# Three of the last stores of a scan-and-adapters kernel, each made by a transfer of 120 and one of 8 partitions

## The chip, the cores and the metric

The kernel runs on one core of one Trainium2 chip. The metric is the time of one execution on the device in microseconds (us); lower is better. The median of three runs of the kernel before is 204.93 us (204.83 to 204.99). Profiles show one execution each.

## The reference

Two steps follow each other. The first is a linear recurrence over time, `h = a*h + b`, for 8 sequences of 6400 steps with 128 channels. Its result, taken as 51200 rows of 128, goes through a mixture of 8 adapters of rank 16, of which each row uses its two best.

```python
def _attn_ref(a, b):                    # a, b: 8 x 6400 x 128
    h = zeros((B, D))
    for t in range(S):
        h = a[:, t] * h + b[:, t]
        out[:, t] = h

def _moe_ref(x, w_gate, A, B):          # x: 51200 x 128, A: 8 x 128 x 16, B: 8 x 16 x 128
    logits = x @ w_gate
    topk = the two largest of the 8 logits;  w = softmax over these two
    delta = sum over the two experts e of  w_e * ((x @ A[e]) @ B[e])
    return x + delta
```

The inputs `a` and `b` are 26.2 MB each and the output is 26.2 MB, so 78.6 MB have to cross between the off-chip and the on-chip memory.

## The kernel before, in words

The 51200 rows are cut into 100 units of 512 rows (`NU = 100`, `UT = 512`). For each unit the `a` and `b` rows are loaded, turned by TensorE so that the channels lie on the 128 partitions (line 81), `a` is copied to the on-chip memory by ScalarE (line 474), and VectorE runs the scan along the free axis (line 493). TensorE then makes the logits and the products with all 8 `A` (line 77), the gates are worked out in groups of units by VectorE and GpSimd, the weighted products are turned and multiplied by `B`, and the sum with `x` in the accumulator `pO` is evicted to the tile `outt` (line 789), by ScalarE alone or, in the last ten units, by ScalarE and VectorE in turn.

`outt` has `NOUT = 24` slots of one unit. A store takes two neighbouring slots, 128 partitions x 2 x 2 KB = 512 KB, to the output; units 98 and 99 have a store of 256 KB each. In the output a unit's 512 rows lie as 128 partitions of 4 rows. There are 51 stores, numbered by the first unit `u0` = 0, 2, ..., 96, 98, 99. The store of `u0` waits for the evictions of its units and, as long as `u0 + HOLD` (20 units later) is under `FREE = 96`, for the scan of that later unit. So the stores run well behind the arithmetic, and at the end some of them are left over.

All loads and stores are issued on SyncE's queue (SP) in an order that a planner (`_Plan.schedule`) makes ahead of time from costs, keys and due times; a step that issues transfers is planned at 450 ns of SP for each transfer that it starts. `add_dma` registers such a step. Its inner `emit` starts the transfers at line 306, and each adds 16 to the semaphore of its slot when it has landed; the slot's semaphore value that users wait for is raised by 16 for each transfer. `_Plan.run` puts a wait at line 193 ahead of each step that needs one. The last instruction of SP, `end`, waits for the last 24 stores.

The line at which a store is described, before the change, is

```python
            rows = out[u0 * UT : (u0 + n) * UT, :].rearrange("(n p i) d -> p n (i d)", p=128, i=Q)
            ...
                [(rows, outt[:, s0 : s0 + n, :])],
```

Of the kernel before, what the change touches and what calls it, by code (L numbers as in the profile page):

```python
# [20 lines left out]
POOL_MULS = (0, 20, 4, 2)  # L21
HOLD = 20
FREE = 96
RING = 8
XR = 16
NOUT = 24
# [173 lines left out]
def bass_associative_scan_2x2__then__mixture_of_adapters_kernel(  # L200
# [20 lines left out]
    lo, hi, every, at = POOL_MULS  # L221
# [23 lines left out]
    with ExitStack() as stack:  # L245
# [11 lines left out]

        a_in = sb(nc.sbuf_tensor("a_in", [128, RING, QI * D], F32))
        b_in = sb(nc.sbuf_tensor("b_in", [128, RING, QI * D], F32))
        a_st = [sb(nc.sbuf_tensor(f"a_st{i}", [128, UT], F32)) for i in range(2)]  # L260
# [5 lines left out]
        outt = sb(nc.sbuf_tensor("outt", [128, NOUT, UT], F32))  # L266
# [30 lines left out]
        def add_dma(name, eng, unit, starts, slot, time, deps=()):  # L297

            if slot not in dma_sem:
                dma_sem[slot] = [sb(nc.semaphore("q_" + "_".join(map(str, slot)))), 0]  # L300
            dma_sem[slot][1] += 16 * len(starts)
            sem, value = dma_sem[slot]

            def emit(h):
                for dst, src in starts:
                    last = h.dma_start(dst, src).then_inc(sem, 16)
                return last

            add(name, eng, "dma", unit, (450.0 * len(starts), 0.0), emit, deps, (sem, value, time))
# [107 lines left out]
        def load(t, w):  # L417

            n = place(t, w)[0]
            many = 1 if (t, w) in alone else 2  # L420
            dst, i = rings[t][:, n % RING, :], QI
            if many == 1:
                dst, i = dst[:, column(t, w) : column(t, w) + UT], Q
            src = rows_of[t][w * UT : (w + many) * UT, :].rearrange("(p i) d -> p (i d)", i=i)
            for k in range(many):
# [3 lines left out]
                "sp",  # L429
                w - 2 * RING + (0 if w > 3 else -200),  # L430
                [(dst, src)],
                (t, n % RING, many, w if many == 1 else 0),
                650.0 if many == 1 else 1265.0,
                users.get((t, n - RING), []),
            )
# [369 lines left out]
        def store(j):  # L805
            u0, n = stores[j]
            s0 = u0 % NOUT
            rows = out[u0 * UT : (u0 + n) * UT, :].rearrange("(n p i) d -> p n (i d)", p=128, i=Q)
            add_dma(
                f"st{j}",  # L810
                "sp",
                u0 + HOLD,
                [(rows, outt[:, s0 : s0 + n, :])],
                ("o", s0, n),
                632.0 * n,
                [f"oev{v}" for v in range(u0, u0 + n)] + [f"scan{u0 + HOLD}"] * (u0 + HOLD < FREE),
            )
# [19 lines left out]
        for j in range(len(stores)):  # L837
            store(j)
# [53 lines left out]
```

## Time and profile before

| what | value |
|---|---|
| median of three runs | 204.93 us (204.83 to 204.99) |
| the profiled execution's own time | 204.77 us |
| its span, first to last instruction | 203.0 us |
| TensorE, VectorE, ScalarE, GpSimd busy | 93%, 91%, 85%, 57% of the span |
| moved by the transfer queues | 79.35 MB, mean 391 GB/s |
| stores | 49 of 512 KB, median 13.2 us from issue to landing; 2 of 256 KB, 4.6 us |
| mean granted TensorE clock | 0.982 |

The span is what the views show; the profiled execution's own time holds 1.8 us more around it. A transfer runs on up to 16 transfer engines side by side, and the DMA share is the mean over all 16, so one engine working alone shows as 0.06. A share can come out slightly over 1, since packets on an engine overlap by a few ns. "From issue to landing" ends with the last of a transfer's 16 landings. L306 and L193 are lines of helpers, so a store is best found by its place in time on SP.

### The profile page before, as it was taken

The numbers are of one execution on the slowest core, as the hardware profiler recorded it, in microseconds if no ns is written. First come the engines' busy times: TensorE is split into PE (matmuls) and PEld (weight loads), VectorE is DVE, ScalarE is ACT, GpSimd is POOL, SyncE is SP. The second block draws the span as 40 slices with busy tenths as digits, with TensorE's granted clock in tenths as the row PEclk, the third lists the DMA queues.
The fourth block names the chain that finished last, engine by engine and source line by source line (L and its number), as shares of the span: only waits on it lengthen the run. The fifth ranks groups of instructions, "written<-read, shape, count | busy, mean of one in ns | idle before, by whom it ended". The sixth has DMA issues, their size and how long they took to land.

```text
span 203.0 us, 8739 instructions
## 1 busy us (share of the span) xinstructions
PE 189.5 (93%) x3594; PEld 167.2 (82%) x3594; DVE 183.8 (91%) x260; ACT 172.8 (85%) x379; POOL 115.4 (57%) x240
## 2 busy tenths in 40 slices
PE   7788899998999999999999999999999999999970
PEld 2567788887889989988899889999998999889960
DVE  1599988999999999999999999999999999999960
ACT  2357498896979999999999999999999999898870
POOL 1326767655758565646656665575775654555610
PEclk9999699999999999999999999999999999999996
DMA  7999999999999999999999999999999999999884
GB/s 184 403 408 407 406 409 402 405 407 408 407 410 413 408 413 416 404 411 408 412 408 415 408 410 409 408 413 411 410 410 411 408 414 409 400 403 358 319 318 151
DMA packets 29671, 79.35 MB, mean 391 GB/s; under 512 B 3648, under 2 KB 3776, under 8 KB 29632
## 3 DMA queue, kind: packets, MB, share of 16 engines
q1 hardware_dynamic: 28304, 78.65, 98.3%
q8 instruction: 29, 0.48, 0.9%
q10 hardware_dynamic: 1328, 0.14, 0.5%
q14 instruction: 10, 0.08, 0.1%
HBM read 52.56 MB, written 26.21 MB: 388 GB/s over the span
## 4 chain that ended last, share of the span: by engine, by line
PE 85%; ACT 7%; DVE 2%; issue 2%
PE pA L81 28%; PE pO L77 22%; PE pTL L81 14%; PE pZ L77 11%; PE pTL L77 5%; PE pB L81 4%; ACT a_st L474 3%; PE pB L77 2%; DVE xT L493 2%; ACT zwT L750 2%; ACT outt L789 2%; ACT z_sb L698 1%; DVE outt L789 0%; ACT g L667 0%; DVE warm_t L355 0%
## 5 line engine op out<-in xcount | busy, mean ns | idle before, releaser
L493 DVE TENSOR_TENSOR_SCAN xT<-a_st,xT,pB 128x512 f16<-128x512 f32 x96 | 120.2, 1252 | 4.5 <-PE pTL L77 1.0
L474 ACT COPY a_st<-pA 128x512 f32<-128x512 f32 x100 | 60.9, 609 | 19.0 <-PE pB L81 15.3
L81 PE MATMUL pA<-ident_f,a_in 64*128 64x64 f32 (+1 forms) x792 | 72.1, 231 | 2.8 <-ACT a_st L474 1.2
L81 PE MATMUL pB<-ident_f,b_in 64*128 64x64 f32 (+1 forms) x792 | 72.6, 231 | 0.2
L81 PEld LDWEIGHTS pA<-ident_f,a_in 64*128 64x128 f32 (+1 forms) x792 | 58.0, 140 | 12.6 <-ACT a_st L474 2.9
L789 ACT COPY outt<-pO 128x512 f32<-128x512 f32 x95 | 59.6, 628 | 1.6 <-PE pO L77 1.4
L81 PEld LDWEIGHTS pB<-ident_f,b_in 64*128 64x128 f32 (+1 forms) x792 | 58.1, 140 | 0.7 <-issue 0.5
L750 ACT COPY zwT<-pTL 128x512 f16<-128x512 f16 x95 | 58.0, 611 | 0.2
L712 DVE TENSOR_TENSOR zw<-pZ,g 128x512 f16<-128x512 f32 x80 | 53.5, 672 | 0.8 <-PE pTL L81 0.2
L77 PE MATMUL pO<-ident_h,xT 128*128 128x128 f16 x400 | 38.6, 220 | 0.7 <-issue 0.3
L77 PE MATMUL pZ<-cst_h,xT 128*128 128x128 f16 x400 | 38.8, 221 | 0.1
L81 PE MATMUL pTL<-ident_h,zw 128*128 128x128 f16 x380 | 38.0, 223 | 0.5 <-issue 0.3
L77 PE MATMUL pO<-cst_h,zwT 128*128 128x128 f16 x400 | 38.1, 217 | 0.3 <-ACT zwT L750 0.3
L712 POOL TENSOR_TENSOR zw<-z_sb,g 128x512 f16<-128x512 f32 x20 | 21.3, 1063 | 17.2 <-PE pTL L77 15.0
L77 PEld LDWEIGHTS pO<-ident_h,xT 128*128 128x128 f16 x400 | 27.8, 114 | 1.8 <-issue 0.6
L77 PE MATMUL pTL<-cst_h,xT 128*128 128x8 f16 x400 | 27.2, 174 | 1.8 <-DVE xT L493 1.8
L77 PEld LDWEIGHTS pZ<-cst_h,xT 128*128 128x128 f16 x400 | 28.2, 114 | 0.4 <-issue 0.3
L81 PEld LDWEIGHTS pTL<-ident_h,zw 128*128 128x128 f16 x380 | 21.9, 98 | 7.0 <-ACT zwT L750 0.7
L77 PEld LDWEIGHTS pTL<-cst_h,xT 128*128 128x128 f16 x400 | 23.3, 116 | 2.7 <-DVE xT L493 2.2
L608 POOL TENSOR_TENSOR d<-Lg,m 128x128 f32<-128x128 f32 (+3 forms) x29 | 10.8, 374 | 25.1 <-DVE m L601 25.1
L77 PEld LDWEIGHTS pO<-cst_h,zwT 128*128 128x128 f16 x400 | 24.0, 97 | 0.9 <-PE pO L77 0.6
L643 POOL TENSOR_SCALAR pn<-d 128x128 f32<-128x128 f32 (+3 forms) x31 | 17.5, 565 | 2.7
(35 smaller groups left out, 137.0 us busy)
## 6 DMA issues: line engine op xcount, KB each, us to landing
a_in<-in_a_dram SPq DMA_DIRECT2D x49, 512.0 KB, 13.6
b_in<-in_b_dram SPq DMA_DIRECT2D x49, 512.0 KB, 13.4
out_dram<-outt SPq DMA_DIRECT2D x49, 512.0 KB, 13.2
a_in<-in_a_dram SPq DMA_DIRECT2D x2, 256.0 KB, 8.0
b_in<-in_b_dram SPq DMA_DIRECT2D x2, 256.0 KB, 4.2
out_dram<-outt SPq DMA_DIRECT2D x2, 256.0 KB, 4.6
cst_f<-in_moe_A_dram ACTq DMA_DIRECT2D x1, 64.0 KB, 3.9
cst_f<-in_moe_B_dram ACTq DMA_DIRECT2D x1, 64.0 KB, 5.0
```

What stands on the lines that cost most here:

```text
L77: return self.h.matmul(*args, **kw)
L81: return self.h.transpose(*args)
L474: lambda h: h.copy(a_st[w % 2][:, :], pA[0][:, :]),
L493: last = h.tensor_tensor_scan(out=x_at(lo, hi), data0=a_st[w % 2][:, lo:hi], data1=pB[w % 2][:, lo:hi], initial=init, op0=ALU.mult, op1=AL ...
L608: lambda h: h.tensor_tensor(out=v(d1[s]), in0=v(Lg[s]), in1=bc(m1[s]), op=ALU.subtract),
L643: lambda h: h.tensor_scalar(v(pn[s]), v(d2[s]), 0.0, -1.0e30, ALU.is_lt, ALU.mult),
L698: lambda h: h.copy(src[:, :], pZ[v % NZ][:, :]),
L712: lambda h: h.tensor_tensor(out=oview, in0=zview, in1=gview, op=ALU.mult),
L750: lambda h: h.copy(zwT[v % 2][:, :], t_dst(v)),
L789: return copy(outt[:, v % NOUT, :], pO[v % NO][:, :])
```

## The change

The stores of `u0` = 88, 90 and 92 are each started as two transfers on SP, one straight behind the other: partitions 0 to 119, then partitions 120 to 127, of the same two slots. The other stores, the waits ahead of each store, the order of the stores and all other work stay. Since two transfers raise the slot's semaphore, `end` waits for 32 more instead of 16 on those three slots, and the planner counts 900 ns of SP for each of the three steps.

```diff
@@ -21,6 +21,7 @@
 HOLD = 20
 FREE = 96
+IN_TWO = (88, 90, 92)
 RING = 8
@@ -805,12 +806,13 @@
         def store(j):
             u0, n = stores[j]
             s0 = u0 % NOUT
+            parts = [(0, 120), (120, 128)] if u0 in IN_TWO else [(0, 128)]
             rows = out[u0 * UT : (u0 + n) * UT, :].rearrange("(n p i) d -> p n (i d)", p=128, i=Q)
             add_dma(
                 f"st{j}",
                 "sp",
                 u0 + HOLD,
-                [(rows, outt[:, s0 : s0 + n, :])],
+                [(rows[lo:hi], outt[lo:hi, s0 : s0 + n, :]) for lo, hi in parts],
                 ("o", s0, n),
                 632.0 * n,
                 [f"oev{v}" for v in range(u0, u0 + n)] + [f"scan{u0 + HOLD}"] * (u0 + HOLD < FREE),
```

## The prediction

> **What bounds the kernel now.** I read the page first, then the stores of the last 18 us one by one, then the transfers after the last arithmetic, because the diff touches only three stores near the end.
>
> ```profile
> span 203.0 us, 8739 instructions
> DMA  7999999999999999999999999999999999999884
> GB/s 184 403 408 407 406 409 402 405 407 408 407 410 413 408 413 416 404 411 408 412 408 415 408 410 409 408 413 411 410 410 411 408 414 409 400 403 358 319 318 151
> q8 instruction: 29, 0.48, 0.9%
> ```
>
> The transfer engines are full, at about 408 GB/s, from the second slice to the 36th; after that the rate falls to 358, 319 and 318. So the body is held by the transfers, and in the last 20 us something else holds most of them back. The q8 line, code being fetched, is 0.9% of 16 engines' 203 us, 29 us of engine time in 29 packets: about 1 us each, and each lies on one engine alone, so engines need not keep step.
>
> The chain of waits ends with the last eviction (line 789), and behind it is only the last store. Below are the last eight stores in order of issue, two lines each: one from the store's instruction (its duration in ns, when it was issued), one with its time from issue to the last of its landings. The first pair is the store of units 86 and 87; the next three are the ones that the change cuts (88, 90, 92); then come 94, 96, 98 and 99.
>
> ```profile
> L306 SPq DMA_DIRECT2D out_dram<-outt x1: 372/372/372, 185.4 to 185.4; - x1
> DMA to landing us min/median/max: 8.8/8.8/8.8
> L306 SPq DMA_DIRECT2D out_dram<-outt x1: 372/372/372, 188.4 to 188.4; - x1
> DMA to landing us min/median/max: 7.3/7.3/7.3
> L306 SPq DMA_DIRECT2D out_dram<-outt x1: 372/372/372, 190.5 to 190.5; - x1
> DMA to landing us min/median/max: 6.5/6.5/6.5
> L306 SPq DMA_DIRECT2D out_dram<-outt x1: 372/372/372, 192.4 to 192.4; - x1
> DMA to landing us min/median/max: 6.0/6.0/6.0
> L306 SPq DMA_DIRECT2D out_dram<-outt x1: 372/372/372, 194.3 to 194.3; - x1
> DMA to landing us min/median/max: 5.3/5.3/5.3
> L306 SPq DMA_DIRECT2D out_dram<-outt x1: 372/372/372, 196.1 to 196.1; - x1
> DMA to landing us min/median/max: 4.7/4.7/4.7
> L306 SPq DMA_DIRECT2D out_dram<-outt x1: 345/345/345, 196.8 to 196.8; - x1
> DMA to landing us min/median/max: 4.7/4.7/4.7
> L306 SPq DMA_DIRECT2D out_dram<-outt x1: 344/344/344, 197.7 to 197.7; - x1
> DMA to landing us min/median/max: 4.4/4.4/4.4
> ```
>
> Adding each pair gives the landings: 194.2, 195.7, 197.0, 198.4, 199.6, 200.8, 201.5 and 202.1. They follow each other by 1.5, 1.3, 1.4, 1.2, 1.2, 0.7 and 0.6 us, although the stores were issued 3.0, 2.1, 1.9, 1.9, 1.8, 0.7 and 0.9 us apart. So whatever lands last works without a pause, at its own pace, and is catching up on a backlog. The next view shows the rest of the transfer engines in the same time (columns: the stretch, its length, the busy time of five engines, granted clock, the DMA share, GB/s).
>
> ```profile
> 188.00:189.30 1.30, 1.18 (x20) 1.03 (x19) 1.01 (x4) 1.30 (x4) 1.00 (x3) 1.00 0.63 243
> 190.60:191.40 0.80, 0.80 (x16) 0.76 (x14) 0.80 (x2) 0.80 (x2) 0.65 (x2) 1.00 0.56 210
> 192.80:193.30 0.50, 0.50 (x12) 0.50 (x11) 0.50 (x2) 0.50 (x2) 0.42 (x2) 1.00 0.50 188
> 194.70:195.20 0.50, 0.50 (x11) 0.45 (x9) 0.50 (x2) 0.50 (x2) 0.00 (x0) 1.00 0.43 164
> 196.60:197.00 0.40, 0.32 (x4) 0.24 (x4) 0.13 (x1) 0.00 (x0) 0.00 (x0) 1.00 0.28 102
> 199.00:199.60 0.60, 0.00 (x0) 0.00 (x0) 0.00 (x0) 0.00 (x0) 0.00 (x0) 0.52 1.04 386
> 199.80:199.90 0.10, 0.00 (x0) 0.00 (x0) 0.00 (x0) 0.00 (x0) 0.00 (x0) 0.50 0.14 41
> 199.90:201.75 1.85, 0.00 (x0) 0.00 (x0) 0.00 (x0) 0.00 (x0) 0.00 (x0) 0.50 0.06 24
> ```
>
> Between one store and the next the share sinks to 0.63, 0.56, 0.50, 0.43, 0.28: most engines have run dry and wait for the arithmetic, while some still work. At 199.0 all 16 are busy, at 199.8 two, and from 199.9 the share is 0.06, which is 1/16. The packets after 199.9 say the same:
>
> ```profile
> GB/s 26 26 26 26 26 26 26 26 26 26 26 26 26 26 26 26 26 26 26 26 26 26 0 0 0 0 0 0 0 0 0 0 0 0 0 0 0 0 0 0
> DMA packets 25, 0.05 MB, mean 15 GB/s; under 512 B 3, under 2 KB 3, under 8 KB 25
> ```
>
> Here 3.1 us are cut in 40 slices: a flat 26 GB/s in 22 of them (1.7 us), made of 22 packets of data and 3 tiny ones. A tiny one closes an engine's part of a store, so one engine alone still owes the end of 96, all of its part of 98 and all of its part of 99. The other fifteen were done by 199.8. **The last 1.7 to 1.9 us of the kernel are one late transfer engine**, and no arithmetic is left.
>
> **The change part by part.**
>
> First, what it takes off. A store of two units is 512 KB; sixteen engines that end together but for one show even shares, 32 KB each, which are 8 of the 128 partitions (4 KB each). One engine alone moves 26 GB/s, so a share is 1.26 us; by the landings above, with the others at work, it is 1.2 to 1.5 us on the late one. A transfer of 120 partitions holds exactly 15 such shares. If it goes over 15 engines, one engine is left out, and three stores relieve it of 3 x 1.26 = 3.8 us or 3 x 1.4 = 4.2 us. No transfer of another shape than 128 partitions stands in this trace, so neither the number of engines nor which one is left out is shown. The two ends are: the late engine is relieved of all three shares, or of none. I take the first: 120 is 15 even shares, the part cut off is the last one in the order of partitions, and an engine that is served last in every transfer is the likeliest to be the last one always, as a single engine is here through nine stores without a pause. That is a judgement, and the chances below say how far I trust it.
>
> [...]
>
> If it is relieved, it ends its share of 86 at the landing at 194.2, and its next work is the store of 94, issued at 194.3. The lateness of 1.9 us is under the 3.8 taken away, so it has caught up by then and takes the last four stores in step with the rest. Two stores (2.5 us) would nearly have done; the third is reserve.
>
> Second, what then ends last. The fifteen ended by about 199.8, the late one 1.8 us later (44 KB at 24 GB/s in the row 199.90:201.75), and its last landing came at 202.1. So the last landing goes to about 200.3. From 202.1 to the span's end are 0.9 us, and from the span of 203.0 to the profiled time of 204.77 another 1.8; neither depends on the stores. Gain of this term: 1.8 us, at most 1.9.
>
> Third, the small transfers of 8 partitions. Each is 32 KB, 0.08 us if spread over 16 engines, 0.16 us a piece if over 8, 1.26 us if on one. Over 8, three of them add 0.5 us to an engine. They fall between 189 and 194, and the first five rows of stretches have on average (0.37 x 1.30) + (0.44 x 0.80) + (0.50 x 0.50) + (0.57 x 0.50) + (0.72 x 0.40) = 1.7 us of idle time per engine from 188.0 on, so most of it is hidden. An engine that had no idle time would show all 0.5. I book 0.1.
>
> Fourth, the issue. SP issues three more transfers, 372 ns each by the rows above. Even with what SP does between two issues, a pair that followed at once, 96 and 98, stood 0.7 us apart. The cut stores and the next one are 1.9 to 2.1 us apart, because SP waits for evictions. So the second issue fits behind the first without moving the next store: nothing, or up to 0.3 us where the small transfer starts late. Nobody but the last instruction waits for these stores (their slots are not written again), and SP has only stores left, so the planner's higher cost of 900 instead of 450 moves no other instruction.
>
> Sum: -1.8 + 0.1 = -1.7 us. On the profiled execution that is 204.77 - 1.7 = 203.07, and on the median of the runs, 0.16 higher, 204.93 - 1.7 = **203.2 us**.
>
> **The rivals.**
>
> *The late engine stays in.* If the part left out is another engine's, the late one keeps its three shares, its backlog and the end at 202.1. The time is then 204.9, or up to 0.5 us more (205.4) if it also takes a part of the small transfers. For it: one engine of sixteen is late, no row names it, and any engine that fetched code more often (1 us each time) could be the one. Against it: only that the part cut off is the last in order. An engine's lateness from fetches would move about with the code, and the landings above show one engine at 1.2 to 1.5 us a share without a change of place.
>
> *The transfers of 120 partitions are slower, and the fifteen become the bound.* [...] Take a doubling: each cut store costs an engine 1.26 us more, 3.8 in three. Less the 1.7 us of idle time this is 2.1 us on the mean engine, or 3.8 on one without idle time. The end of the fifteen goes from 200.3 to 202.4, up to 204.1: the time is 205.2 to 206.9, slower. It decides from (1.8 + 1.7)/3 = 1.2 us more per cut store on a mean engine, 0.6 us on one with no idle time. [...] Nothing in the trace has the new shape.
>
> [...]
>
> **How the numbers follow.** The forecast has 0.73. The late engine that stays in has 0.15, of which 0.08 lies within 0.2% (0.4 us, about what a measurement of this kernel can tell from no change) and 0.07 above. The slower transfers of 120 have 0.12. So faster 0.73, same 0.08, slower 0.19. The forecast's own bounds: 1.9 us gained with the runs' scatter of 0.1 gives 202.9; a loss of 0.5 for the small transfers, 0.3 for a late start and a partial slowing give about 204.4. To leave out no more than 2 in 10 the range must take in the unchanged time and a bit above: 202.9 to 205.2.
>
> **What would show it.** Right: in the changed profile the stretch of 0.06 at the end is gone or under 0.4 us, the last landing comes about 2.6 us after the last store's issue instead of 4.4, and the store of 94 lands within 3.3 us of its issue instead of 5.3. The three small transfers show as separate issues of SP about 0.4 us behind their large ones, and the last store is still issued 197.7 us into the span. Wrong: the 26 GB/s tail is still there at 1.7 us or more (the late engine was not the one left out), or the last stores start behind full engines, with a share of 1 between stores from 189 to 197 where the rows above show 0.28 to 0.63 (the cut stores are slow). A tail of some 0.5 us would mean that the relief is right and the small transfers, or the second latest engine, end last.

## The result, and the profile after

The changed kernel is slower: median 205.54 us (205.2 to 206.43) against 204.99 us for the kernel before in the same measurement, a ratio of 1.003 with a 95% interval of 1.0015 to 1.0044. That is 0.55 us more, where 1.7 us less was forecast.

The page of the changed kernel, rate of the transfers in 40 slices of 5.1 us:

```profile
GB/s 173 401 412 405 406 410 403 405 406 412 406 408 413 410 414 412 404 412 410 411 408 414 407 413 409 408 413 410 417 407 407 414 411 406 400 395 336 280 280 171
```

This profiled execution took 206.06 us, 0.5 above its median, so its span of 204.3 us (203.0 before) overstates the loss. The body is as before; the last slices carry less, 336, 280 and 280 GB/s where the kernel before had 358, 319 and 318.

The stores one by one, as in the prediction: an issue and its time to landing. First the store of 84, two ahead of the first cut store (kernel before, then changed), then 94, 96, 98 and 99 of the changed kernel.

```profile
L306 SPq DMA_DIRECT2D out_dram<-outt x1: 372/372/372, 182.4 to 182.4; - x1
DMA to landing us min/median/max: 10.5/10.5/10.5
```

```profile
L307 SPq DMA_DIRECT2D out_dram<-outt x1: 372/372/372, 183.0 to 183.0; - x1
DMA to landing us min/median/max: 10.7/10.7/10.7
L307 SPq DMA_DIRECT2D out_dram<-outt x1: 1177/1177/1177, 195.0 to 195.0; - x1
DMA to landing us min/median/max: 5.9/5.9/5.9
L307 SPq DMA_DIRECT2D out_dram<-outt x1: 979/979/979, 196.8 to 196.8; - x1
DMA to landing us min/median/max: 5.4/5.4/5.4
L307 SPq DMA_DIRECT2D out_dram<-outt x1: 802/802/802, 197.8 to 197.8; - x1
DMA to landing us min/median/max: 5.0/5.0/5.0
L307 SPq DMA_DIRECT2D out_dram<-outt x1: 1142/1142/1142, 198.6 to 198.6; - x1
DMA to landing us min/median/max: 4.7/4.7/4.7
```

The store of 84 lands at 193.7 where it was 192.9: this execution was 0.8 us behind before any cut store (its store of 84 was also issued 0.6 us later). From there the last landing is 9.6 us on (203.3); before it was 9.2 us (202.1). The store of 94 was to land within 3.3 us of its issue and took 5.9, the last one was to take 2.6 and took 4.7. And SP is held 0.8 to 1.2 us at each of the last four, where the same four issues took 0.34 to 0.37 us before; the last store is issued at 198.6, 0.9 us later.

The stretches, in the columns of the prediction, first the five between stores, then the end:

```profile
188.00:189.30 1.30, 1.30 (x25) 1.23 (x23) 1.01 (x4) 1.30 (x5) 0.80 (x3) 1.00 0.70 268
190.60:191.40 0.80, 0.80 (x17) 0.77 (x15) 0.80 (x3) 0.80 (x2) 0.50 (x2) 1.00 0.91 269
192.80:193.30 0.50, 0.50 (x12) 0.47 (x10) 0.50 (x3) 0.50 (x3) 0.24 (x1) 1.00 0.90 266
194.70:195.20 0.50, 0.50 (x13) 0.50 (x10) 0.50 (x2) 0.50 (x3) 0.00 (x0) 1.00 0.69 188
196.60:197.00 0.40, 0.30 (x5) 0.26 (x4) 0.32 (x1) 0.40 (x2) 0.00 (x0) 1.00 0.91 317
201.00:202.00 1.00, 0.00 (x0) 0.00 (x0) 0.00 (x0) 0.00 (x0) 0.00 (x0) 0.50 0.38 143
202.20:203.00 0.80, 0.00 (x0) 0.00 (x0) 0.00 (x0) 0.00 (x0) 0.00 (x0) 0.50 0.06 23
```

The last row is one lone engine again, 0.06 and 23 GB/s: one engine still ends last. But it is alone for only about 1.0 us (202.0 to 203.0) where it was 1.85. The row above it goes with that: most of the other fifteen end between 201.0 and 202.0, where they had ended by 199.9. The first five rows show a second thing. The engines are busier (0.91, 0.90, 0.69, 0.91 where it was 0.56, 0.50, 0.43, 0.28), yet they move little for it: packets take longer. The same stretch of 6 us, kernel before, then changed:

```profile
190.00:196.00 6.00, 6.00 (x97) 5.40 (x94) 5.33 (x11) 5.33 (x13) 2.70 (x9) 1.00 0.87 328
```

```profile
190.00:196.00 6.00, 6.00 (x100) 5.57 (x98) 5.96 (x12) 5.10 (x12) 3.18 (x11) 1.00 0.85 255
```

Nearly the same share moves 255 GB/s in place of 328. A packet of a store holds 2048 bytes, so share x 16 x 2048 / rate is 87 ns for a packet before and 109 ns after.

### The profile page after: what moved, and what is told of

Same layout as the page of the kernel before. It is cut to its first block, busy times and chain, and to the rows that moved or that the text cites. A ratio compares the mean times of both kernels' runs of the same rounds, so it can differ in the third digit from the quotient of the medians.

```text
span 204.3 us, 8742 instructions
## 1 busy us (share of the span) xinstructions
PE 190.0 (93%) x3594; PEld 167.5 (82%) x3594; DVE 183.8 (90%) x260; ACT 172.8 (85%) x379; POOL 115.1 (56%) x240
## 4 chain that ended last, share of the span: by engine, by line
PE 84%; ACT 8%; DVE 2%; issue 2%; DVEq 0%
PE pA L82 28%; PE pO L78 21%; PE pTL L82 14%; PE pZ L78 11%; PE pTL L78 5%; PE pB L82 4%; ACT a_st L475 3%; PE pB L78 2%; ACT zwT L751 2%; DVE xT L494 2%; ACT outt L790 2%; ACT z_sb L699 1%; DVE outt L790 0%; ACT g L668 0%; DVE warm_t L356 0%
```

## The experiments

Two causes were open. Theory A: the late engine was not the one left out by the transfer of 120 partitions, keeps its 8 partitions of each large transfer, and takes a part of the small one too. Theory B: the extra issues hold SP, and the last store starts later. All kernels are the changed one with other stores or other cuts, in the line

```diff
-            parts = [(0, 120), (120, 128)] if u0 in IN_TWO else [(0, 128)]
+            parts = [...] if u0 in IN_TWO else [(0, 128)]
```

**Cut, but in even parts.** 112 and 16 partitions, both for sixteen engines, at 88, 90 and 92.

```diff
+            parts = [(0, 112), (112, 128)] if u0 in IN_TWO else [(0, 128)]
```

> The same three stores (88, 90, 92) cut at partition 112 instead of 120: transfers of 112 and of 16 partitions, both of which divide into 16 even parts (7 and 1 partitions). So no engine is left out and none gets more than in one transfer of 128; only the three extra issues on SP are left. Theory A (the late engine keeps its 8 partitions in the large transfer and gets a part of the small one as well, 0.2 us three times): the last landing is not delayed by the late engine, and the time is that of the kernel before, at most 0.2 us above: 205.0 to 205.2. Theory B (the cost is the issue: SP is held at the extra transfers, 0.8 to 1.5 us where the kernel before shows 0.37, and the last store starts later): the time is that of the changed kernel, 205.4 to 205.6, and the issues of SP after the cut stores take 0.8 to 1.5 us again.

Measured: 205.08 us against 204.98, ratio 1.001 (1.0001 to 1.0019). Three extra issues cost 0.1 us and not 0.55. The page counts 48 packets under 512 B more than the kernel before (3696, 3648), the tiny ones that close an engine's part: 16 more for each of the three stores, so no engine is left out of either transfer. The packets are slow here too, in the row below (105 ns by the same sum), so slow packets alone don't set the end either. They do eat into the lead of the other engines: the last row shows 3.0 us from 200.1 on in 40 slices, and 27 GB/s, one engine, stands without a break from 200.9 to 201.7 only, 0.8 us in place of 1.85.

```profile
190.00:196.00 6.00, 6.00 (x101) 5.56 (x99) 5.65 (x12) 5.17 (x12) 2.95 (x10) 1.00 0.92 288
GB/s 301 191 164 109 82 55 55 82 55 27 55 27 27 27 27 27 27 27 27 27 27 0 0 0 0 0 0 0 0 0 0 0 0 0 0 0 0 0 0 0
```

So theory A stands, and the question is which engine is late.

**The small rest in 7 and 1.**

```diff
+            parts = [(0, 120), (120, 127), (127, 128)] if u0 in IN_TWO else [(0, 128)]
```

> The three stores in three transfers each, of 120, 7 and 1 partitions. If a transfer takes the largest number of engines up to 16 that divides its partitions, in order from the first, the 7 go to the first seven engines and the 1 to the first. Theory A with the late engine as the eighth: it gets no small part any more, and the 0.6 us go: 204.9 to 205.2. Theory A with the late engine among the first seven: as the changed kernel or 0.1 us above (205.5 to 205.7). Theory B (issue on SP): six extra issues instead of three, so the loss about doubles: 205.9 to 206.2.

Measured: 205.63 us against 204.98, ratio 1.0035 (1.0021 to 1.0048), the loss of the changed kernel. The issues doubled and the loss did not; by the expectation, the late engine is one of the seven that share the 7.

**119 and 9, one store.** At 88, and in a second kernel at 86.

```diff
-IN_TWO = (88, 90, 92)
+IN_TWO = (88,)
+            parts = [(0, 119), (119, 128)] if u0 in IN_TWO else [(0, 128)]
```

> One store alone (88) cut in transfers of 119 and 9 partitions: 119 is 7 times 17, so seven engines would carry 17 partitions each and the 9 go one each to nine engines. If the late engine is the eighth, it has 1 partition of this store instead of 8 and is relieved of 7/8 of 1.4 us: the time falls by 1.0 to 1.2 us, 203.8 to 204.0. If it is one of the first seven, it carries 18 instead of 8 and gets 1.6 us more: 206.5 to 206.7. Theory B (only the issue costs): one extra issue, 205.0 to 205.2 with the 26 GB/s tail of one engine as before.

> As with the store 88, but the store of 86, one earlier, so that the seven engines with 17 partitions have one more gap between stores in which to catch up. Late engine the eighth: down by 1.0 to 1.3 us, 203.7 to 204.0, no worse than at 88. Late engine among the first seven: 206.5 to 206.7. Theory B: 205.0 to 205.2.

Measured: 206.76 us (ratio 1.0086, 1.0072 to 1.01) and 206.71 us (1.008, 1.0067 to 1.0094) against 204.98: 1.8 and 1.7 us more with a single extra issue, which rules out theory B. It is near the 1.6 us expected of a late engine with 17 partitions of the large transfer and one of the small one. The page counts 3648 packets under 512 B, as many as with the store uncut: the two transfers have 16 parts together, as 7 and 9 would. The loss is the same with one more gap between stores to catch up in, as it would be for an engine that has no idle time. If the 119 go over the first seven engines, all from the eighth on are ruled out, with them the one that the prediction wanted to relieve.

**Parts of 6, 5, 4, 3 and 2.**

```diff
+IN_TWO = {86: (0, 120, 126, 128), 88: (0, 120, 125, 128), 90: (0, 120, 124, 128)}
+            cut_at = IN_TWO.get(u0, (0, 128))
+            parts = list(zip(cut_at[:-1], cut_at[1:]))
```

> Which of the first seven engines is late. Three stores in three transfers each: 86 in 120, 6 and 2 partitions, 88 in 120, 5 and 3, 90 in 120, 4 and 4. If a transfer of n under 16 partitions goes one each to the first n engines, an engine numbered from 0 takes part in so many of the six small transfers: number 6 in none, 5 in one, 4 in two, 3 in four, 2 in five, 1 or 0 in six; each part costs the late engine about 0.2 us. So the loss against the kernel before is 0.0 to 0.1 us for number 6, 0.2 for 5, 0.4 for 4, 0.8 for 3, 1.0 for 2, 1.2 for 1 or 0. Rival (the loss goes by the number of issues on SP, six more here as with 120, 7 and 1): 0.65 us.

Measured: 205.32 us against 204.97, 0.35 more, ratio 1.0029 (1.0012 to 1.0047). It is nearest to number 4 (counted from 0, so the fifth), but the interval, 0.25 to 0.96 us, takes in number 3 and the rival's 0.65 as well, and in its trace other engines had fallen back too; by itself it settles nothing. I misread it at first and took number 6 (next but one).

**The other way round.** Partitions 0 to 7 first, then 8 to 127.

```diff
+            parts = [(0, 8), (8, 128)] if u0 in IN_TWO else [(0, 128)]
```

> The stores 88, 90, 92 cut the other way round: partitions 0 to 7 first, then 8 to 127. If engines are given out by their order and not by the place in the on-chip memory, the small transfer lies on the same first eight engines and the late one is among them: as the changed kernel, 205.4 to 205.7. If each engine belongs to its partitions, the rows now left out are those of another engine, and the time differs from the changed kernel: below 205.0 if that is the late one, and no small part for it if it is not.

Measured: 205.55 us against 204.97, ratio 1.0023 (1.0006 to 1.0039). Which partitions are cut off makes no difference to the loss (0.58 us, 0.55 in the changed kernel), as expected if engines are given out by their order and not by the place in the on-chip memory.

**114 and 14.** At 86 alone, at 82 and 86, at 86 and 90.

```diff
+IN_TWO = (86,)
+            parts = [(0, 114), (114, 128)] if u0 in IN_TWO else [(0, 128)]
```

> The store of 86 alone, cut in 114 and 14 partitions. 114 is 6 times 19, so the large transfer would lie on the first six engines with 19 partitions each, and the 14 go one each to the first fourteen. The cut 119 and 9 (first seven engines) cost 1.7 us, so the late engine is one of the first seven. Theory: it is the seventh, number 6, since in the run with parts of 6, 5, 4, 3 and 2 the last engine seemed to take none. Then it carries 1 partition instead of 8 and the last landing comes 7 x 0.176 = 1.2 us earlier: 203.7 to 204.0. Rival: it is one of the first six; it then carries 20 instead of 8, and the time is 2.1 us above the kernel before, 206.9 to 207.1.

> The same cut on the stores 82 and 86. If number 6 is the late engine it is relieved twice (2.4 us) and is no longer last; the six engines with 20 partitions get 2 x 1.9 us more against some 2 to 3 us in which they ran dry. Theory: the end is set by these six, between 203.0 and 204.0, so no worse than one store alone or up to 0.7 us better. Rival (late engine among the first six): 4.2 us slower, about 209.

> The same cut on 86 and 90, the second one 4.3 us nearer to the end. If number 6 is the late engine, it is relieved of 2.4 us as with 82 and 86, but the six engines have less time left to catch up with the second: 203.6 to 204.8, worse than 82 and 86. Rival: about 209.

Measured: 206.98 us (ratio 1.0109, 1.0095 to 1.0123), 210.03 us (1.0248, 1.0228 to 1.0267) and 209.78 us (1.0234, 1.0204 to 1.0265) against 204.91. My theory (number 6) fell and the rival's 2.1 us came to the tenth: by the expectation the late engine is among the first six. Its issue and landing of the last store, and the lone engine behind it:

```profile
L307 SPq DMA_DIRECT2D out_dram<-outt x1: 1121/1121/1121, 197.8 to 197.8; - x1
DMA to landing us min/median/max: 6.2/6.2/6.2
```

```profile
200.30:203.50 3.20, 0.00 (x0) 0.00 (x0) 0.00 (x0) 0.00 (x0) 0.00 (x0) 0.50 0.07 26
```

One engine works alone for 3.2 us now; the other fifteen have caught up, although by the expectation five of them carried 20 partitions of that store too. With two stores the loss is 5.1 and 4.9 us, 0.7 to 0.9 more than the 4.2 of the rival; what the rest is stays open.

**68 and 60.** By the expectation four engines with 17, fifteen with 4.

```diff
+IN_TWO = (86,)
+            parts = [(0, 68), (68, 128)] if u0 in IN_TWO else [(0, 128)]
```

> The store of 86 alone in transfers of 68 and 60 partitions. 68 is 4 times 17: four engines with 17 partitions; 60 is 15 times 4: fifteen engines with 4. The cut 114 and 14 (six engines) cost 2.1 us, so the late engine is one of the first six; in the run with parts of 6, 5, 4, 3 and 2 the loss was 0.35 us, two parts of 0.2, which is number 4. Theory: number 4 (or 5) is late and has 4 partitions of this store instead of 8, so the last landing comes 4 x 0.176 = 0.7 us earlier: 204.1 to 204.4; the four engines with 21 partitions get 2.0 us more, about what they have in idle time. Rival: the late engine is one of the first four, carries 21 instead of 8 and the time is 2.3 us longer, 207.2.

Measured: 204.34 us against 204.93, ratio 0.9972 (0.996 to 0.9983): 0.6 us faster than the kernel before, inside the 204.1 to 204.4 that were forecast. It beats both kernels. Its last store and the end:

```profile
L307 SPq DMA_DIRECT2D out_dram<-outt x1: 350/350/350, 197.7 to 197.7; - x1
DMA to landing us min/median/max: 3.9/3.9/3.9
```

```profile
200.00:200.80 0.80, 0.00 (x0) 0.00 (x0) 0.00 (x0) 0.00 (x0) 0.00 (x0) 0.50 0.13 51
```

The last landing takes 3.9 us from issue instead of 4.4, and the tail has two engines side by side (0.13, 51 GB/s): a second one has come up almost level with the late one. By the sum it is one of the four loaded ones; the trace does not name it. So little more is to be expected this way. The next kernel cuts two stores like that, 82 and 86.

> The same cut on 82 and 86. If number 4 or 5 is late it is relieved of 1.4 us, 203.5 to 203.8, unless the first four engines with 13 partitions more in each of two stores (4.1 us) now end last: then 204.5 to 206. If the late engine is one of the first four: 209.5.

Measured: 205.97 us against 204.93, ratio 1.0051 (1.0035 to 1.0068). The second relief is more than eaten up, inside the 204.5 to 206 of the condition on the first four engines.

**95 and 33.**

```diff
+            parts = [(0, 95), (95, 128)] if u0 in IN_TWO else [(0, 128)]
```

> Number 4 or number 5. The store of 86 in transfers of 95 and 33 partitions: 95 is 5 times 19, the first five engines; 33 is 11 times 3. If the late engine is number 4, it carries 22 partitions instead of 8, 14 x 0.176 = 2.5 us more: 207.2 to 207.6. If it is number 5, it carries 3 instead of 8, 0.9 us less: 203.9 to 204.4.

Measured: 207.11 us against 204.89, ratio 1.0108 (1.0092 to 1.0125): number 4, a little under the 207.2 to 207.6 forecast for it and far from number 5. All runs together, as partitions that number 4 carries more or less than in uncut stores, at 0.176 us each (that price is the mean of the two runs of 119 and 9, so their row agrees by construction). Measured are differences of medians:

| cut | partitions | by the sum, us | measured, us |
|---|---|---|---|
| 112 + 16, three stores | 0 | 0.0 | +0.10 |
| 120 + 8, three stores (the change) | +3 | +0.5 | +0.55 |
| 8 + 120, three stores | +3 | +0.5 | +0.58 |
| 120 + 7 + 1, three stores | +3 | +0.5 | +0.65 |
| 120 + parts of 6 to 2 | +2 | +0.35 | +0.35 |
| 119 + 9, one store | +10 | +1.8 | +1.78, +1.73 |
| 114 + 14, one store | +12 | +2.1 | +2.07 |
| 95 + 33, one store | +14 | +2.5 | +2.22 |
| 68 + 60, one store | -4 | -0.7 | -0.59 |
| 114 + 14, two stores | +24 | +4.2 | +5.12, +4.87 |
| 68 + 60, two stores | -8 | -1.4 | +1.04 (others end last) |

The first nine rows follow the sum within 0.25 us, both in sign and in size, with one late engine, the fifth in order, and with the numbers of engines that the expectations suppose: 4 for a transfer of 68 partitions, 5 for 95, 6 for 114, 7 for 119, 15 for 120, each with even parts. For some of the cuts the pages count the parts, by the packets under 512 B that close them. In order: the kernel before, the changed one, 112 and 16, 119 and 9 (at 88), 95 and 33, and 120, 7 and 1.

```profile
DMA packets 29671, 79.35 MB, mean 391 GB/s; under 512 B 3648, under 2 KB 3776, under 8 KB 29632
DMA packets 29692, 79.35 MB, mean 388 GB/s; under 512 B 3669, under 2 KB 3797, under 8 KB 29653
DMA packets 29719, 79.35 MB, mean 391 GB/s; under 512 B 3696, under 2 KB 3824, under 8 KB 29680
DMA packets 29671, 79.35 MB, mean 388 GB/s; under 512 B 3648, under 2 KB 3776, under 8 KB 29632
DMA packets 29671, 79.35 MB, mean 386 GB/s; under 512 B 3648, under 2 KB 3776, under 8 KB 29632
DMA packets 29695, 79.35 MB, mean 390 GB/s; under 512 B 3672, under 2 KB 3800, under 8 KB 29656
```

Counted from 16 for an uncut store, one for each engine, a cut one has 23 parts in the changed kernel (21 packets more on three stores; 15 and 8 were supposed), 32 with 112 and 16, 16 with 119 and 9 (7 and 9) and 16 with 95 and 33 (5 and 11). With 120, 7 and 1 it has 24 where 15, 7 and 1 make 23; for which of the three the supposed number is wrong is not shown. For 68 and 114 only the times speak. The trace names no engine: "number 4" is a place in that order, found by these sums. The steps that found it ran on four different chips, with the kernel before at 204.89 to 204.98 us on each; that one place fits them all speaks against a fault of a single chip.

## Why the prediction was wrong

The reading of the kernel was right: the last 1.8 us are one late transfer engine, and what it carries in the last stores sets the time, at 0.176 us a partition; the prediction's 1.4 us for 8 is 0.175.

The step that failed is "what it takes off": of its two ends I took "relieved of all three shares". The late engine was relieved of none: by the sums it carries 3 partitions more, 0.5 us, and the loss is 0.55. My reason, that an engine served last in every transfer is the likeliest to be last always, has nothing behind it in these runs. The lone engine was shown, which one it is was not, and 0.73 was far too much for a guess over sixteen. The numbers of engines, 15 for 120 and 8 for 8, agree with the 23 parts counted for a cut store, and with the fifth engine as the late one they would have given the loss.

A second step, "what then ends last", would have failed too. It left the other fifteen at 199.8, untouched by the cut. In the changed kernel's profile most of them end between 201 and 202. A lone engine is left for about 1.0 us there, 0.8 us with 112 and 16, 0.6 us with 8 and 120, 0.4 us with the parts of 6 to 2, and 1.6 us or more (27 GB/s from 200.7 on) only with 120, 7 and 1 (one execution each). An estimate from these: with the right engine left out, three cut stores would in four of the five have gained at most 0.4 to 1.0 us, not 1.8.

The first rival is what happened: it stays in and takes a part of the small transfers. It was priced at up to 0.5 us, "205.4"; the measured loss is 0.55 and the median 205.54. I spread 0.07 of chance on it where it needed most of it, and my range ended at 205.2.

The second rival, slow transfers of 120, happened too, in part: packets take 109 ns in place of 87 between 190 and 196. The idle time hid it only in part, and the rest fell into the lead of the fifteen, so that the end hardly shows it: with 112 and 16 packets are about as slow and the loss is 0.1 us. The late engine's own packets cannot have been slowed alike. It has no idle time, and 18 ns more (105 less 87) for each of its 48 packets of three stores would be 0.9 us, an estimate.

The small transfers: booked at 0.1 us because most engines have idle time there. The late engine has none, the very case for which I named 0.5, and it is the one that counts. That 0.5 took eight engines for a transfer of 8, which no run had shown; the 23 parts of a cut store and the loss of 0.55 us agree with it. The issues were booked at nothing: about right, 0.1 us with three more. The 372 ns an issue behind it did not hold: SP is held 0.8 to 1.2 us at the last four issues. Issues that long stand in the kernel before as well, in its full body (2.38 us for the store at 126.6). They delay the start of the last stores, but the late engine still works on older ones then.

What stays open: why number 4 is the late one. It was behind before the stores shown: in the kernel before, the time from issue to landing falls from 10.5 us (store of 84) to 4.4 (the last one), so at the end the late engine only catches up. No run here says when it fell back or what slowed it.

## What to carry to other kernels

A lone busy engine behind the last arithmetic (a share of 1/16, a flat rate) is a real reserve, but a relief needs the engine's name, and a trace without names gives it only by experiment: cuts of different divisors, one store each, found it by sign and size, together with a supposed number of engines for each transfer that the times, and for some cuts the packet counts, agree with. A change that spreads work should be priced on the engine that ends last, with no idle time to hide in, not on the mean engine. Of the 1.8 us only 0.6 was had with the cuts tried here, since by those numbers the work that 68 and 60 take from the fifth engine falls on the four ahead of it: with two stores cut so, the time was 1.04 us longer.

## What the runs showed of the hardware that I had not expected

Cutting stores of 128 partitions in two makes the packets in flight slower on average, even when all sixteen engines keep even parts: in the same 6 us 87 ns a packet uncut, 105 with 112 and 16, 109 with 120 and 8. The slow time goes with the cut stores: with only the store of 86 cut, in 114 and 14, the same 6 us are at 88 ns (a share of 0.88 at 328 GB/s), and in the changed kernel the packets are back at 88 ns from 198 to 199 (1.02 at 381 GB/s), when all engines are busy but mostly uncut stores are left. Why is not shown.

And the lateness of one engine is so even that it can be measured: over six measurements on several chips the median of the kernel before stays within 204.89 to 204.99 us, so that medians of 4 to 12 runs told losses some tenths of a us apart. Only one execution of the kernel before was profiled; that the same engine is late in the others is inferred from the sums.
